# A new opening list and fewer one-column steps in a fused attention, SoLU and PReLU kernel

## Chip, cores and metric

The kernel runs on one core of one Trainium2 chip. The metric is the device time of one execution in microseconds (us). The kernel before takes 1259.91 us, the median of three runs (1259.33 to 1259.91).

## What is computed

Eight batches of eight heads, 576 positions, 64 values per head. Attention is local: each head's positions are cut in chunks of 64, and a chunk attends only to itself. Then come two dense blocks over the 4608 tokens.

```
scores = scale * q_c @ k_c^T ; attn = exp(scores - max) ; attn /= (sum(attn) + 1e-9)
x   = (attn @ v_c)  laid out as 4608 tokens x 512
h   = x @ w_in (512 x 1024) ; e = exp(h - max(h)) ; solu = h * e / (sum(e) + 1e-9)
y   = (solu - mean) / sqrt(var + 1e-6) * g_ln @ w_out (1024 x 512)
h2  = y @ w_in2 (512 x 2048) ; out = (max(h2,0) + alpha * min(h2,0)) @ w_out2 (2048 x 512)
```

## The kernel before

Each float32 product is made from rounded high parts and remainders (low parts): high x high, high x low and low x high, three matmuls. The program has two phases. Phase 1 goes over 36 token tiles of 128 and does attention, the SoLU block and the normalisation, and writes y to DRAM. Phase 2 does the second dense block, with sums of blocks in place of some of the products.

All work is issued in an order written out by hand, and each engine runs its own instructions in that order. A two-letter or one-letter name stands for one step and the number behind it for the tile or weight unit. `FIRST` is the list for the opening, up to tile 10 or so; after it `STEP` is repeated for each tile, and `LAST` drains phase 1 into phase 2. The steps that matter here, with engine and line:

- `q`, `v` load a tile (SP queue; `q` is held back until the `qk` that frees its buffer was issued, 3 buffers; `v` likewise). `f` fetches a weight unit. The weights come as 64-bit numbers; a unit is 128 x 512 of them. Units 0 to 7 are w_in, 8 to 15 are w_out, the later ones belong to phase 2.
- Conversion of unit u: `p` (ACT, L147 and L148, two activations of 128x512), `s`/`S` (subtract, L153), `l` (DVE, L159 then L162), `a`/`A` (add, L348), `h` (ACT, high part, L356, or L363 and L364), `o`/`O` (low part, L368). A small letter puts `s`, `a` and `o` on GpSimd (POOL), a capital on VectorE (DVE).
- Attention of tile i: `qk` (PE, 32 small matmuls, L381), `qm` (DVE, max L390 and subtraction L392), `qe` (ACT, exp in place, L397), `qs` (DVE: sum over 64 columns L401, plus 1e-9 L402, reciprocal L403), `qn` (e times the reciprocal, L408; on POOL for i < 12, else on DVE), `tr` (PE transposes, L415), `te` (ACT copy out of PSUM, L420), `pv` (PE, L436), `xh` (ACT, L448), `xl` (DVE, L453).
- SoLU of tile i: `hm` (PE, 24 matmuls of 512 columns, L462 and L468, into the only PSUM buffer of its kind), `hx` (DVE, max over 1024, L476), `he` (ACT, exp with the sum, L482), `so` (DVE: plus 1e-9 L487, reciprocal L488, product with the sum over the row L490, and -sum/1024 L493), `sq` (ACT, square with bias and sum, L498), `zv` (DVE, one column, L503), `pw` (POOL, power -0.5, L509), `zs` (DVE, 128x1024, L513), `zt` (PE transposes, L524), `zh` (ACT, L538), `zl` (DVE, L544).
- `ya`, `yb` (PE, L169 to L171): the second product in blocks of 12 matmuls; `ye`, `yx` copy results out (ACT, L571) and store them.

`hm` of the next tile can't start before `so` (L490) has read the PSUM buffer. The first `hm` needs all eight units of w_in: their high parts `h` and their low parts `o`, the low parts in the order in which its matmuls use them.

Of the kernel before, what the change touches and what calls it, by code (L numbers as in the profile page):

```python
# [1171 lines left out]
```

## Time and profile before

| | |
|---|---|
| median of three runs | 1259.91 us |
| profiled execution: its own time | 1258.6 us |
| profiled execution: span, first to last instruction | 1256.7 us |
| PE busy | 1223.2 us, 97% of the span |
| VectorE (DVE) busy | 926.9 us, 74% |
| ScalarE (ACT) busy | 674.9 us, 54% |
| GpSimd (POOL) busy | 324.1 us, 26% |

The profile is that of one execution, 1.3 us under the median. Busy time is the time in which an engine has an instruction in flight. Two instructions of one engine can overlap a little at their ends, so the start of one to the start of the next (a step, below) is what an instruction costs its engine. Stretches are given in us from the start of the span.

### The profile page before, as it was taken

To read this page: it belongs to the slowest core of one execution; us is meant where nothing else is said; L and a number is where in the kernel's file an instruction comes from. 1 tells how busy PE (TensorE), PEld (TensorE's weight loads), DVE (VectorE), ACT (ScalarE), POOL (GpSimd) and SP (SyncE) were. 2 spreads that over 40 slices of the span, in tenths; PEclk is the share of its full clock that TensorE was granted. 3 is DMA by queue.
4 is the path that set the end of the run, shared out by engine and by line. 5 is a ranking of instruction groups with operands and counts; after the bars stand their busy time and mean duration, and the time that the engine had idled before them with its cause. 6 is when DMAs were issued, how large, how long until landed. Compare 5 with 4: busy or idle time off the path is not lost.

```text
span 1256.7 us, 20820 instructions
## 1 busy us (share of the span) xinstructions
PE 1223.2 (97%) x7830; PEld 1058.8 (84%) x7830; DVE 926.9 (74%) x1345; ACT 674.9 (54%) x1061; POOL 324.1 (26%) x299
## 2 busy tenths in 40 slices
PE   5789999999999999999999999999999999999998
PEld 4678888888888888888888899988888888889998
DVE  7986577777877777436776777777885977859594
ACT  6685455555555555335665656666634444434442
POOL 4665145544646555233011020300000000000000
PEclk9899999999999999999999999999999999999999
DMA  8453356564745643468653445469993837547463
GB/s 329 152 158 110 102 175 184 167 197 141 243 162 186 225 168 135 146 266 329 232 201 122 153 174 164 166 233 316 327 349 119 286 112 243 179 138 246 140 213 101
DMA packets 148276, 244.63 MB, mean 195 GB/s; under 512 B 14672, under 2 KB 81360, under 8 KB 147664
## 3 DMA queue, kind: packets, MB, share of 16 engines
q1 hardware_dynamic: 145872, 241.22, 56.1%
q10 hardware_dynamic: 2304, 2.10, 0.5%
q8 instruction: 61, 1.00, 0.3%
q14 instruction: 39, 0.32, 0.1%
HBM read 154.93 MB, written 88.34 MB: 194 GB/s over the span
## 4 chain that ended last, share of the span: by engine, by line
PE 73%; issue 10%; POOL 9%; DVE 4%; ACT 3%; DMA 1%; DVEq 0%; POOLq 0%; ACTq 0%
PE ov L1010 8%; PE oz L1010 8%; PE ox L1010 8%; PE hv L767 7%; PE hx L767 7%; PE hz L767 7%; PE h L462 6%; PE oy L1010 4%; PE hy L767 3%; PE yps L169 3%; PE yps L171 3%; PE yps L170 3%; POOL lo L236 3%; PE h L468 3%; POOL a L153 2%
## 5 line engine op out<-in xcount | busy, mean ns | idle before, releaser
L806 DVE SCALAR_TENSOR_TENSOR g<-ng,nal,g 128x512 f32<-128x512 f32 (+1 forms) x160 | 117.5, 734 | 51.2 <-ACT g L679 49.5
L679 ACT ACTIVATE ng<-g 128x512 f32<-128x512 f32 (+1 forms) x120 | 70.8, 590 | 121.6 <-DVE g L673 121.1
L169 PE MATMUL yps<-zz,wo_h 128*128 128x512 f32 x288 | 115.2, 400 | 0.0
L171 PE MATMUL yps<-zz,wo_l 128*128 128x512 f32 x288 | 112.4, 390 | 0.0
L170 PE MATMUL yps<-zz,wo_h 128*128 128x512 f32 x288 | 112.2, 389 | 0.0
L767 PE MATMUL hv<-th,w 128*128 128x512 f32 (+1 forms) x320 | 104.9, 368 | 0.4 <-DVE g L673 0.3
L767 PE MATMUL hz<-th,w 128*128 128x512 f32 (+1 forms) x320 | 104.7, 368 | 0.4 <-DVE g L673 0.3
L767 PE MATMUL hx<-th,w 128*128 128x512 f32 (+1 forms) x320 | 104.7, 368 | 0.2 <-ACT g L679 0.2
L1010 PE MATMUL ov<-rhi,w 128*128 128x512 f32 (+3 forms) x308 | 93.1, 364 | 0.0
L1010 PE MATMUL oz<-rhi,w 128*128 128x512 f32 (+1 forms) x304 | 92.8, 366 | 0.0
L1010 PE MATMUL ox<-rhi,w 128*128 128x512 f32 (+1 forms) x304 | 92.8, 366 | 0.0
L679 ACT ACTIVATE rhi<-rt 128x1024 fp32r<-128x1024 f32 (+1 forms) x56 | 53.8, 969 | 62.0 <-DVE rt L676 16.8
L676 POOL TENSOR_TENSOR yt<-y,y 128x512 f32<-128x512 f32 (+1 forms) x20 | 25.8, 1310 | 216.7 <-DMA y<-yd 216.7
L676 DVE TENSOR_TENSOR rlo<-rt,rhi 128x1024 fp32r<-128x1024 f32 (+1 forms) x56 | 61.3, 1107 | 15.5 <-ACT rhi L679 15.4
L679 ACT ACTIVATE g<-g 128x512 f32<-128x512 f32 (+1 forms) x120 | 70.3, 586 | 2.6
L462 PE MATMUL h<-wi_h,xh 128*128 128x512 f32 x256 | 68.9, 391 | 0.0
L462 PE MATMUL h<-wi_l,xh 128*128 128x512 f32 x256 | 68.7, 390 | 0.0
L767 PEld LDWEIGHTS hv<-th,w 128*128 128x128 f32 x320 | 59.6, 188 | 9.1 <-issue 0.8
L767 PEld LDWEIGHTS hz<-th,w 128*128 128x128 f32 x320 | 59.6, 188 | 8.5 <-DVE g L673 1.0
L767 PEld LDWEIGHTS hx<-th,w 128*128 128x128 f32 x320 | 59.6, 188 | 8.1 <-ACT g L679 0.6
L498 ACT ACTIVATE eh<-sl,st 128x1024 f32<-128x1024 f32 x36 | 41.5, 1152 | 45.5 <-DVE st L493 45.5
L171 PEld LDWEIGHTS yps<-zz,wo_l 128*128 128x128 f32 x288 | 54.0, 188 | 11.8
(175 smaller groups left out, 3212.9 us busy)
## 6 DMA issues: line engine op xcount, KB each, us to landing
gd<-g SPq DMA_DIRECT2D x96, 256.0 KB, 3.1
qkt<-in_qk SPq DMA_DIRECT2D x36, 512.0 KB, 5.2
w<-wod SPq DMA_DIRECT2D x28, 448.0 KB, 5.0
gd<-g SPq DMA_DIRECT2D x64, 192.0 KB, 1.8
raw<-in_moe_w_out SPq DMA_DIRECT2D x24, 511.8 KB, 4.2
rc<-gd SPq DMA_DIRECT2D x22, 512.0 KB, 4.1
rd<-gd SPq DMA_DIRECT2D x22, 512.0 KB, 4.9
vt<-in_v SPq DMA_DIRECT2D x36, 256.0 KB, 4.8
```

The costliest lines, as they stand in the source:

```text
L169: nc.tensor.matmul(o, lh, rh, start=first, stop=False)
L170: nc.tensor.matmul(o, lh, rl, start=False, stop=False)
L171: nc.tensor.matmul(o, ll, rh, start=False, stop=last)
L236: nc.gpsimd.tensor_tensor(out=lo[:, :w], in0=f, in1=hi[:, :w].bitcast(F32), op=ALU.subtract)
L462: nc.tensor.matmul(ps[:, n], xh[:, kk], w[:, kk, 512 * n:512 * n + 512], start=(kk == 0 and w is wi_h), stop=False,)
L468: nc.tensor.matmul(ps[:, n], xl[:, kk], wi_h[:, kk, 512 * n:512 * n + 512], start=False, stop=(kk == K1 - 1),)
L498: nc.scalar.activation(out=e, in_=s, func=AF.Square, bias=st[:, 4:5], accum_out=st[:, 5:6])
L676: eng.tensor_tensor(out=out, in0=a, in1=b, op=ALU.subtract)
L679: nc.scalar.activation(out=out, in_=in_, func=func, **k)
L767: nc.tensor.matmul(self.ps[x], w[:, a, i, k], d[:, k], start=(p not in CHAINED and k + j == 0), stop=(k == 1 and j == 2), skip_group_check ...
L806: nc.vector.scalar_tensor_tensor(out=self.g[t], in0=self.n[t], scalar=nal_sb[:, f:f + 1], in1=self.g[t], op0=ALU.mult, op1=ALU.add)
L1010: nc.tensor.matmul(bank[key, m][:, e:f], W[2 * j + k][:, a, i, 128 * m:128 * m + 128], d[:, k, e:f], start=(p not in CHAINED and j + k + q ...
```

## The change

- `qs`: exp now writes its 64 columns per head into one of two tiles with 65 columns per head, whose last column was set to 1e-9 once. The sum goes over 65 columns, and the addition L402 is gone.
- `qn` reads that tile and writes the old one. The list says which engine: `qn` POOL, `QN` DVE. The opening list has `QN0` and `qn1` to `qn11`, `STEP` has `QN`, so only tile 0 changes engine. `qe` of a tile has to come behind `qn` of the tile two before.
- `so`: L487 now also multiplies by 1024, so that the sum of L490 is the mean, up to a power of two; L493 is gone, `sq` takes its bias straight from L490, and a new one-column POOL instruction behind `sq` makes the mean for `zs`. The factor 32 x 1024 that is then missing is put into the copy of `ye`.
- `zv` is one addition instead of a multiplication and an addition, in one instruction as before.
- Buffers: `q` has four instead of three, e of SoLU two tiles instead of one (odd tiles use the new one, on the left side of SBUF), and the two 65-column tiles are new.
- A new opening list, with the same 412 entries up to capitals. `s` on DVE: 15 instead of 8 (in the opening), `a` 8 instead of 7, `o` of units below 16: 9 instead of 4.

Lists and diff are cut behind the first `ya`:

```diff
--- before.py
+++ after.py
@@ -51,28 +51,28 @@
 FIRST_TILES = 10
 FIRST = order(
     """
-    q0 f0 p0 q1 qk0 f1 q8 qk1 qm0 f3 qe0 q9 f2 p1 qs0 s0 qn0 tr0 te0 l0 v0 a0 q2 pv0 q12 qm1 f5 p3 q7 S1
-    qe1 qk2 l1 q3 A1 f4 v1 qs1 p2 S2 h1 qm2 xh0 q4 v2 l2 h0 p5 qe2 s3 xl0 v4 qk3 qn1 o0 qs2 O1 a2 f8 p4
-    qm3 qn2 l3 tr1 v7 f7 f6 te1 h2 tr2 q5 qe3 pv1 a3 S4 v3 f10 xh1 qs3 qk4 o2 qn3 te2 p7 qm4 qe4 pv2 S5
-    l4 h16 tr3 l5 A4 xh2 q6 qs4 te3 a5 p6 s7 xl2 f9 xl1 qk5 qm5 p8 h4 v8 v5 h5 qn4 h3 s6 O4 tr4 f11 qe5
-    l6 te4 qs5 pv4 A6 xh4 l7 f12 pv3 xh3 qk6 qn5 A7 h6 h7 o6 xl3 v6 o5 qm6 o7 O3 qe6 s8 tr5 te5 xl4 qs6
-    l8 a8 hm0 p9 qn6 p10 s10 hx0 g0 qk7 qk8 he0 qm7 s9 qe7 so0 p11 l9 tr6 q10 qs7 hm1 qm8 pv5 qn7 sq0 h8
-    te6 l10 qe8 p12 zv0 qk9 a10 qs8 f13 pw0 a9 hx1 zs0 he1 s11 pv6 so1 qm9 xh5 xh6 sq1 tr7 s12 te7 xl5
-    zt0 zv1 h10 hm2 pw1 l12 f14 zh0 p13 l11 zs1 zl0 hx2 qe9 a11 pv7 a12 S13 qn8 f15 qk10 al0 zt1 o8 h11
-    o11 o10 he2 p14 tr8 so2 q11 qs9 sq2 S14 zv2 zh1 l14 pw2 f16 h9 zs2 hm3 f18 zl1 v11 a14 p15 hx3 qn9
-    l13 xl6 f21 a13 te8 h12 f17 zt2 he3 zh2 f19 p16 f20 tr9 so3 h13 zl2 sq3 qm10 hm4 s15 pv8 qk11 te9
-    l15 s16 xh7 zv3 h14 A15 p18 pw3 s18 o16 O13 o14 l16 h15 o9 hx4 o12 he4 zs3 o15 zt3 so4 sq4 zh3 l18
-    zv4 qe10 p17 zl3 A16 hm5 s17 hx5 ya1 he5 l17 yb1 so5 sq5 ye1 hm6 p19 a17 ya0 qs10 zv5 pw4 h18 xl7
...
+    q10 q0 qk0 qm0 f1 p1 f0 qe0 qs0 QN0 p0 q1 f3 S0 l0 s1 l1 qk1 a1 q2 v0 f2 qm1 v7 p3 qe1 q3 tr0 te0 p2
+    qk2 f5 h1 v4 f4 S3 A0 qs1 qm2 h16 q4 pv0 l3 S2 qn1 f6 qe2 qk3 f7 q8 l2 h0 xh0 p4 qs2 v1 a2 q12 qm3
+    tr1 te1 a3 v2 qe3 xl0 qk4 qs3 v8 v3 p5 qm4 q5 qn2 f9 h2 S4 O1 q6 S5 tr2 qe4 p6 pv1 te2 l5 o0 xh1 qn3
+    f8 l4 tr3 p7 pv2 q7 f10 A4 h4 o4 A5 S7 S6 q11 qs4 qk5 o2 qn4 xl1 te3 xh2 xl2 qm5 l7 l6 p9 tr4 qk6 h5
+    te4 qe5 A7 a6 q9 h3 qs5 h7 g0 h6 f11 p8 pv3 qm6 O6 xh3 f12 O5 qe6 f14 O7 f13 pv4 xh4 O3 v5 S8 qn5
+    xl4 l8 hm0 tr5 qs6 a8 qk7 hx0 qk8 qn6 te5 s9 qm7 he0 qe7 so0 l9 O17 a9 qs7 qm8 p10 tr6 sq0 p11 zv0
+    f16 qn7 hm1 te6 pw0 pv5 S10 S11 l10 h8 qe8 zs0 p12 hx1 v6 qk9 he1 S12 l12 so1 zt0 l11 al0 qm9 xh5
+    a10 h9 sq1 qs8 xl3 tr7 hm2 xl5 h10 zh0 o8 f17 zv1 a12 te7 zl0 a11 p14 qe9 pv6 pw1 pv7 hx2 qn8 p13
+    he2 tr8 s14 zs1 s13 so2 qk10 zt1 h12 l14 qm10 qs9 sq2 l13 a13 zv2 p16 zh1 zl1 te8 pw2 h11 hm3 hx3
+    he3 zs2 qn9 h18 f15 so3 p15 xh7 zt2 tr9 f18 sq3 S15 A14 zh2 zv3 pw3 l15 h14 zl2 h13 te9 hm4 s16 zs3
+    hx4 he4 xl7 A15 so4 qk11 l16 h15 O15 xh6 v9 pv8 zt3 h17 o13 o10 O9 f20 hm5 p18 sq4 o11 S18 zh3 xl6
+    v10 zl3 zv4 hx5 he5 so5 O14 p17 O12 ya1 qe10 ya2 sq5 f19 hm6 v11 S17 xh8 pw4 l17 a16 l18 f21 zs4 zv5
...
     """
 )
 STEP = order(
     """
     q+3 v+3 ye-6 zh-2 zl-2 conv+0 hm+0 tr+1 te+1 qk+2 hx+0 he+0 qm+2 qe+2 pv+1 zt-1 so+0 sq+0
-    ya-5 xh+1 xl+1 zv+0 pw+0 conv+1 qs+2 zs+0 qn+2 yb-5 yx-5
+    ya-5 xh+1 xl+1 zv+0 pw+0 conv+1 qs+2 zs+0 QN+2 yb-5 yx-5
     """
 )
 TWICE = {20, 26, 31}
@@ -174,13 +174,13 @@
         with ExitStack() as c1, ExitStack() as c0:
             L = lambda name, bufs, **k: c0.enter_context(tc.tile_pool(name=name, bufs=bufs, side="left", **k))
             R = lambda name, bufs, **k: c1.enter_context(tc.tile_pool(name=name, bufs=bufs, side="right", **k))
-            qkp = L("qk", 3)
+            qkp = L("qk", 4)
...
-            ep = R("e", 1)
+            ep = R("e", 1), L("f", 1)
@@ -194,7 +194,7 @@
 -            frees = {"q": ("qk", 3), "v": ("pv", 3)}
+            frees = {"q": ("qk", 4), "v": ("pv", 3)}
 
             def load_q(i):
                 t = qs[i] = qkp.tile([128, 2, 2, 2, 2, CH], F32, name="qkt", tag="qk")
@@ -368,6 +368,9 @@
                 eng.tensor_tensor(out=units[u][2] if u < UI else wo["l"][:, u - UI], in0=f, in1=hi.bitcast(F32), op=ALU.subtract)
 
             sc, ee, att, xs, hs = {}, {}, {}, {}, {}
+            exs = [at.tile([128, H, CH + 1], F32, name=f"ex{k}", tag=f"ex{k}", bufs=1) for k in range(2)]
+            for ex in exs:
+                nc.gpsimd.memset(ex[:, :, CH:CH + 1], 1e-9)
             ss, zz_, pvs, rs = {}, {}, {}, {}
 
             def qk(i):
@@ -393,19 +396,22 @@
                 ee[i, 0] = e
 
             def qexp(i):
+                assert i < 2 or ("qn", i - 2) in done
                 e = ee[i, 1] = ee.pop((i, 0))
-                nc.scalar.activation(out=e, in_=e, func=AF.Exp, scale=scale)
+                nc.scalar.activation(out=exs[i % 2][:, :, 0:CH], in_=e, func=AF.Exp, scale=scale)
 
             def qsum(i):
+                assert ("qe", i) in done
                 r = sm.tile([128, H], F32, name="r", tag="r", bufs=3)
-                nc.vector.tensor_reduce(out=r, in_=ee[i, 1], op=ALU.add, axis=AX.X)
-                nc.vector.tensor_scalar(out=r, in0=r, scalar1=1e-9, scalar2=None, op0=ALU.add)
+                nc.vector.tensor_reduce(out=r, in_=exs[i % 2], op=ALU.add, axis=AX.X)
                 nc.vector.reciprocal(out=r, in_=r)
                 rs[i] = r
 
-            def qnorm(i):
+            def qnorm(i, eng):
                 e, r = ee[i, 1], rs.pop(i)
-                (nc.gpsimd if i < 12 else nc.vector).tensor_tensor(out=e, in0=e, in1=r.unsqueeze(2).to_broadcast([128, H, CH]), op=ALU.mult)
+                eng.tensor_tensor(
+                    out=e, in0=exs[i % 2][:, :, 0:CH], in1=r.unsqueeze(2).to_broadcast([128, H, CH]), op=ALU.mult
+                )
 
             def tr(i):
                 assert i not in rs
@@ -478,30 +484,34 @@
 
             def hexp(i):
                 st = ss.pop((i, 0))
-                e = ep.tile([128, FF1], F32, name="eh", tag="eh")
+                e = ep[i % 2].tile([128, FF1], F32, name="eh", tag="eh")
                 nc.scalar.activation(out=e, in_=hs[i], func=AF.Exp, bias=st[:, 0:1], accum_out=st[:, 1:2])
                 ss[i, 1] = st, e
 
             def solu(i):
                 st, e = ss.pop((i, 1))
-                nc.vector.tensor_scalar(out=st[:, 2:3], in0=st[:, 1:2], scalar1=1e-9, scalar2=None, op0=ALU.add)
+                nc.vector.tensor_scalar(
+                    out=st[:, 2:3], in0=st[:, 1:2], scalar1=1e-9, scalar2=float(FF1), op0=ALU.add, op1=ALU.mult
+                )
                 nc.vector.reciprocal(out=st[:, 2:3], in_=st[:, 2:3])
                 s = sp.tile([128, FF1], F32, name="sl", tag="sl")
                 nc.vector.scalar_tensor_tensor(
                     out=s, in0=hs.pop(i), scalar=st[:, 2:3], in1=e, op0=ALU.mult, op1=ALU.mult, accum_out=st[:, 3:4]
                 )
-                nc.vector.tensor_scalar(out=st[:, 4:5], in0=st[:, 3:4], scalar1=-1.0 / FF1, scalar2=None, op0=ALU.mult)
                 ss[i, 2] = st, e, s
 
             def square(i):
                 st, e, s = ss.pop((i, 2))
-                nc.scalar.activation(out=e, in_=s, func=AF.Square, bias=st[:, 4:5], accum_out=st[:, 5:6])
+                nc.scalar.activation(
+                    out=e, in_=s, func=AF.Square, scale=-float(FF1), bias=st[:, 3:4], accum_out=st[:, 5:6]
+                )
+                nc.gpsimd.tensor_scalar(out=st[:, 4:5], in0=st[:, 3:4], scalar1=1.0 / FF1, scalar2=None, op0=ALU.mult)
                 ss[i, 3] = st, s
 
             def zvar(i):
                 st, s = ss[i, 4] = ss.pop((i, 3))
                 nc.vector.tensor_scalar(
-                    out=st[:, 6:7], in0=st[:, 5:6], scalar1=1.0 / FF1, scalar2=1e-6, op0=ALU.mult, op1=ALU.add
+                    out=st[:, 6:7], in0=st[:, 5:6], scalar1=1e-6 * FF1, scalar2=None, op0=ALU.add
                 )
 
             def zpow(i):
@@ -511,7 +521,7 @@
             def zscale(i):
                 st, s = ss.pop((i, 5))
                 nc.vector.tensor_scalar(
-                    out=s, in0=s, scalar1=st[:, 4:5], scalar2=st[:, 7:8], op0=ALU.add, op1=ALU.mult
+                    out=s, in0=s, scalar1=st[:, 4:5], scalar2=st[:, 7:8], op0=ALU.subtract, op1=ALU.mult
                 )
                 zz_[i] = s
 
@@ -568,7 +578,7 @@
 
             def ystore(j, m):
                 y = yp.tile([128, YG], F32, name="ysb", tag="ysb")
-                nc.scalar.activation(out=y, in_=ypend.pop((j, m)), func=AF.Copy)
+                nc.scalar.activation(out=y, in_=ypend.pop((j, m)), func=AF.Copy, scale=32.0 * FF1)
                 pairs = (0, 1) if Z_SLOTS[j][0][0] < Z_SLOTS[j][1][0] else (1, 0)
                 for c, p in enumerate(pairs):
                     t0 = j * YG + p * YP
@@ -594,21 +604,21 @@
             nc.gpsimd.memset(b64[:, 0:1], -8.0 * 896 * 16)
             nc.gpsimd.memset(b64[:, 1:2], -8.0 * (896 + 2048) * 16)
             nc.gpsimd.memset(mhalf, -0.5)
-            nc.scalar.activation(out=mhalf, in_=mhalf, func=AF.Copy)
+            nc.scalar.activation(out=b64, in_=b64, func=AF.Copy)
             make_identity(nc, ident)
...
-                qk=qk, qm=qmax, qe=qexp, qs=qsum, qn=qnorm, tr=tr, te=tevac, pv=pv, xh=xhigh, xl=xlow,
+                qk=qk, qm=qmax, qe=qexp, qs=qsum, qn=lambda i: qnorm(i, nc.gpsimd), QN=lambda i: qnorm(i, nc.vector), tr=tr, te=tevac, pv=pv, xh=xhigh, xl=xlow,
...
```

## Rows read from the trace of the kernel before

**Rows 1.** Windows: engines' busy time in stretches, granted TensorE clock, DMA

```profile
0.00:43.50 43.50, 24.04 (x408) 21.41 (x409) 32.89 (x61) 26.59 (x44) 20.24 (x26) 0.88 0.77 285
...
80.00:90.00 10.00, 6.79 (x30) 5.49 (x29) 9.76 (x19) 9.54 (x17) 4.62 (x5) 0.83 0.40 122
...
101.36:560.00 458.64, 456.47 (x3580) 384.88 (x3579) 320.74 (x531) 243.70 (x395) 222.41 (x208) 1.00 0.52 174
```

Columns: stretch and its length; busy time and (x instructions) of PE, PE weight loads, DVE, ACT and POOL; granted TensorE clock as a share of full speed; share of the DMA engines' time; GB/s.

**Rows 2.** Timeline of PE: where the `hm` groups and the first `ya` begin

```profile
43.50 1.17 PE L462 MATMUL h<-wi_h,xh 128*128 128x512 f32 x4
...
53.70 1.21 PE L462 MATMUL h<-wi_h,xh 128*128 128x512 f32 x4
...
74.17 1.16 PE L462 MATMUL h<-wi_h,zz 128*128 128x512 f32 x4 [1.04 <-DVE sl L490]
...
84.40 2.04 PE L462 MATMUL h<-wi_h,zz 128*128 128x512 f32 x4 [3.21 <-DVE sl L490]
...
95.83 1.15 PE L462 MATMUL h<-wi_h,zz 128*128 128x512 f32 x4 [1.09 <-DVE sl L490]
...
101.36 0.39 PE L169 MATMUL yps<-zz,wo_h 128*128 128x512 f32 x1
```

Columns: start, duration, engine, line, operation, output and inputs, shape, number merged; in brackets the idle time before it and what ended it.

**Rows 3.** Timeline: the links between the first and second `hm`

```profile
49.46 1.23 DVE L476 TENSOR_REDUCE st<-h 128x1 f32<-128x1024 f32 x1 [0.17 <-PE h L468]
...
50.72 1.11 ACT L482 ACTIVATE eh<-h,st 128x1024 f32<-128x1024 f32 x1 [1.14 <-DVE st L476]
...
52.35 1.28 DVE L490 SCALAR_TENSOR_TENSOR sl<-h,st,eh 128x1024 f32<-128x1024 f32 x1
```

**Rows 4.** Windows: the stretch from the first `qm` to the first `hx`

```profile
7.30:49.46 42.16, 28.02 (x402) 24.05 (x404) 38.55 (x69) 28.20 (x48) 24.14 (x21) 0.88 0.72 274
```

**Rows 5.** Timeline of DVE in the opening

```profile
16.35 0.70 DVE L402 TENSOR_SCALAR r<-r 128x8 f32<-128x8 f32 x1
...
17.20 0.39 DVE L153 TENSOR_TENSOR a<-pos,neg 128x512 bf16<-128x512 bf16 x1
17.51 0.68 DVE L390 TENSOR_REDUCE nm<-sc 128x8 f32<-128x512 f32 x1
18.22 0.69 DVE L392 TENSOR_TENSOR e<-sc,nm 128x512 f32<-128x512 f32 x1
18.83 1.04 DVE L159 TENSOR_SCALAR g<-a 128x512 uint16<-128x512 uint16 x1
19.91 0.69 DVE L162 SCALAR_TENSOR_TENSOR f<-wrawh,g 128x512 f32<-128x512 uint32 x1
20.52 0.68 DVE L453 TENSOR_TENSOR xl<-xd,xh 128x512 fp32r<-128x512 f32 x1
21.12 0.68 DVE L401 TENSOR_REDUCE r<-e 128x8 f32<-128x512 f32 x1
21.83 0.17 DVE L402 TENSOR_SCALAR r<-r 128x8 f32<-128x8 f32 x1
22.03 0.20 DVE L403 RECIPROCAL r<-r 128x8 f32<-128x8 f32 x1
22.15 0.64 DVE L368 TENSOR_TENSOR wi_l<-f,wi_h 128x512 fp32r<-128x512 f32 x1
...
24.14 0.28 DVE L159 TENSOR_SCALAR g<-a 128x512 uint16<-128x512 uint16 x1
```

**Rows 6.** Timeline of POOL beside the first row of Rows 5

```profile
15.87 1.16 POOL L153 TENSOR_TENSOR a<-pos,neg 128x512 bf16<-128x512 bf16 x1 [2.29 <-DVE f L348]
```

**Rows 7.** Waits of PE up to 101 us: who waited for whom, total, times, longest

```profile
PE et L415 <- POOL e L408: 8.0, 4, 4.4
```

**Rows 8.** Timelines of SP, ACT and PE around the start of phase 2

```profile
525.79 2.03 SPq L724 DMA_DIRECT2D y<-yd  x4
...
529.66 1.15 ACT L498 ACTIVATE eh<-sl,st 128x1024 f32<-128x1024 f32 x1 [2.00 <-DVE st L493]
...
559.69 0.39 PE L767 MATMUL hx<-y,w 128*128 128x512 f32 x1
```

More of the change, by code (lines that the diff above doesn't have):

```diff
@@ L64 @@
-    l15 s16 xh7 zv3 h14 A15 p18 pw3 s18 o16 O13 o14 l16 h15 o9 hx4 o12 he4 zs3 o15 zt3 so4 sq4 zh3 l18
-    zv4 qe10 p17 zl3 A16 hm5 s17 hx5 ya1 he5 l17 yb1 so5 sq5 ye1 hm6 p19 a17 ya0 qs10 zv5 pw4 h18 xl7
-    zs4 xh8 pw5 f22 hx6 zt4 zh4 he6 yb0 zs5 a18 zt5 zl4 h19 ya2 xl8 hm7 p20 so6 S19 zh5 s20 ye0 v9 sq6
-    zl5 zv6 pw6 pv9 zs6 hx7 he7 so7 p21 sq7 zt6 yb2 zh6 hm8 v12 v10 xh9 h17 zv7 xl9 l19 o18 hx8 pw7 zl6
-    qn10 tr10 a19 zs7 qm11 o17 te10 he8 ya3 yb3 zt7 so8 pv10 sq8 zh7 zl7 hm9 l20 f23 ya4 zv8 hx9 S21 ye3
@@ L69 @@
-    he9 pw8 ye2 yx3 xh10 A20 zs8 so9 sq9 qe11 zv9 qs11 pw9 xl10 qn11 zs9 yb4 zt8
+    q10 q0 qk0 qm0 f1 p1 f0 qe0 qs0 QN0 p0 q1 f3 S0 l0 s1 l1 qk1 a1 q2 v0 f2 qm1 v7 p3 qe1 q3 tr0 te0 p2
+    qk2 f5 h1 v4 f4 S3 A0 qs1 qm2 h16 q4 pv0 l3 S2 qn1 f6 qe2 qk3 f7 q8 l2 h0 xh0 p4 qs2 v1 a2 q12 qm3
+    tr1 te1 a3 v2 qe3 xl0 qk4 qs3 v8 v3 p5 qm4 q5 qn2 f9 h2 S4 O1 q6 S5 tr2 qe4 p6 pv1 te2 l5 o0 xh1 qn3
+    f8 l4 tr3 p7 pv2 q7 f10 A4 h4 o4 A5 S7 S6 q11 qs4 qk5 o2 qn4 xl1 te3 xh2 xl2 qm5 l7 l6 p9 tr4 qk6 h5
@@ new lines @@
+    he3 zs2 qn9 h18 f15 so3 p15 xh7 zt2 tr9 f18 sq3 S15 A14 zh2 zv3 pw3 l15 h14 zl2 h13 te9 hm4 s16 zs3
+    hx4 he4 xl7 A15 so4 qk11 l16 h15 O15 xh6 v9 pv8 zt3 h17 o13 o10 O9 f20 hm5 p18 sq4 o11 S18 zh3 xl6
+    v10 zl3 zv4 hx5 he5 so5 O14 p17 O12 ya1 qe10 ya2 sq5 f19 hm6 v11 S17 xh8 pw4 l17 a16 l18 f21 zs4 zv5
+    hx6 he6 yb1 pw5 zs5 xl8 zt4 ya0 ye1 zh4 A17 so6 a18 hm7 yb0 zl4 qs10 o18 zt5 qm11 p19 sq6 ye0 pv9
+    hx7 zv6 pw6 zh5 he7 p20 zs6 zl5 yb2 qn10 so7 zt6 hm8 ya3 ye2 sq7 yb3 zh6 zv7 S19 pw7 l19 s20 xh9 zl6
@@ L70 @@
+    hx8 xl9 he8 zs7 tr10 p21 qe11 zt7 zh7 l20 so8 qs11 hm9 sq8 te10 f22 pv10 h19 zv8 pw8 zl7 hx9 yx3 he9
+    v12 ya4 zs8 so9 a19 xh10 zt8 ye3 xl10 o16 qn11 sq9 zv9 pw9 s21 A20 zs9 yb4 f23
     """
@@ L119, in tile_chunk_attention_solu_prelu @@
     al_sb = const.tile([128, KF2], F32, name="al_sb")
-    mhalf = const.tile([128, 1], F32, name="mhalf")
-    b64 = const.tile([128, 2], F32, name="b64")
+    b64 = const.tile([128, 3], F32, name="b64")
+    mhalf = b64[:, 2:3]
     y_dram = [dram.tile([128, K1, 2 * n], F32, name=f"yd{j}") for j, (_, n) in enumerate(GROUP)]
@@ L196, in phase1 @@
             done = set()
-            frees = {"q": ("qk", 3), "v": ("pv", 3)}
+            frees = {"q": ("qk", 4), "v": ("pv", 3)}
             def load_q(i):
@@ L610, in phase1 @@
             top = dict(
-                {k: TILES for k in "q v qk qm qe qs qn tr te pv xh xl hm hx he so sq zv pw zs zt zh zl ya yb ye yx".split()},
+                {k: TILES for k in "q v qk qm qe qs qn QN tr te pv xh xl hm hx he so sq zv pw zs zt zh zl ya yb ye yx".split()},
                 **{k: len(units) for k in "fpsla"}, **{k: UO for k in "hoO"}, S=len(units), A=len(units), g=1, al=1,
```

## Prediction, made before the changed kernel was run

> **What bounds the kernel now.** The windows come first [rows 1]: up to 43.5 us PE is busy 24.04 us only, so it idles 19.5; from 80 to 90 it idles 3.2; from 101.36 to 560, 458.64 us, it idles 2.2. So behind the first `ya` PE's own work sets the pace, and that work is the same in both kernels. What the change can win or lose is the time of the fifth `hm` interval's end, 95.83, or of the first `ya`, 101.36 [rows 2]; from there every microsecond is carried to the end, and nothing else on DVE, ACT or POOL shows.
>
> Next, the timeline of PE [rows 2]: the `hm` groups of tiles 0 to 5 begin at 43.50, 53.70, (the third not shown,) 74.17, 84.40 and 95.83: 10.2, twice 10.2, 10.2 and 11.4 us. The links [rows 3] say what an interval is: `hm` itself 5.7 to 6.0 (43.50 to 49.46), from `hx` to `he` 1.26, to the product of `so` 1.63, to the next `hm` 1.35. That is a loop through one PSUM buffer, PE to DVE to ACT to DVE to PE. A change that takes none of these four instructions away can't make it much shorter than 10.2. So the opening has two parts: A, how soon the first `hm` ends and `hx` starts (49.46), and B, five intervals (46.4 us).
>
> Part A is set by DVE. From its first instruction at 7.30 to `hx` at 49.46 DVE is busy 38.55 of 42.16 us [rows 4], and `hx` starts 0.17 us behind the end of `hm`: both were late together. PE's waits in that stretch are for POOL's `qn` (8.0 us [rows 7]), which is filled from DVE in turn.
>
> **Step prices on DVE.** From start to start, undisturbed [rows 5]: `S` 0.31 (17.20 to 17.51), `qm` 0.71 + 0.61, `l` 0.31 + 0.61 (L159 takes 0.28 and 0.03 to the next), `xl` 0.60, `qs` 0.71 + 0.20 + 0.12, of which L402 is the 0.20. I take `A` and `QN` at 0.61 like L162 and `O` at 0.60 like `xl`, all operations on 512 float32 columns.
>
> Some are disturbed. L402 at 16.35 takes 0.70, not 0.17, and ends at 17.05, when POOL's subtraction (15.87 plus 1.16 [rows 6]) ends; L159 at 18.83 takes 1.04 instead of 0.28 [rows 5]. So some DVE instructions wait for the POOL instruction in flight. The Trainium skill (SBUF — State Buffer, Who interferes with whom) says the same and more: a DVE instruction with two inputs in SBUF, too, shares a port with GpSimd, and whichever starts first keeps it for its whole length. By that rule every `S`, `A`, `O` and `QN` that is moved to DVE is one more candidate to wait; the sum with that stands among the rivals, worked out from L402's row.
>
> **Part A, list against list.** Ahead of `hx0` the old list has on DVE 7 `qm`, 7 `qs`, 9 `l`, 4 `S`, 4 `A`, 3 `O`, 5 `xl`: 9.24 + 7.21 + 8.28 + 1.24 + 2.44 + 1.80 + 3.00 = 33.2 us. The new one has 7 `qm`, 7 `qs` (now 0.83), 9 `l`, 8 `S`, 4 `A`, 5 `O`, 4 `xl` and `QN0`: 9.24 + 5.81 + 8.28 + 2.48 + 2.44 + 3.00 + 2.40 + 0.61 = 34.3. DVE gets 1.05 us more to do, since 4 `S`, 2 `O` and `QN0` outweigh L402 seven times. (65 columns instead of 64 are a sixty-fourth of 0.71, 0.01 each.)
>
> So the gain has to come from the waits. Before they were 42.16 - 33.2 = 9.0 us: 3.6 idle (42.16 - 38.55), the other 5.4 inside of instructions, behind POOL. POOL has 21 instructions in this stretch [rows 4]; the new list leaves it 14: `s0`, `s3`, `s6`, `s7`, `s8`, `a0`, `a5`, `qn0`, `o5`, `o6`, `o7` go to DVE or behind `hx0`, and `s1`, `a1`, `o4`, `a6` come. Two estimates, from above and below:
> - Waits behind POOL fall with the count, 14/21, and the idle time stays: 34.3 + 3.6 + 3.6 = 41.5, `hx0` at 48.8.
> - Walking down the new list entry by entry with these prices, 1.16 for a POOL instruction [rows 6] and somewhat over half of 1.15 for an ACT instruction of 512 columns (1.15 is one of 1024 [rows 8]), DVE waits in four places only: for the first exp 0.7 (as before), for `qk2` 0.35, for `qe3` 0.15, `S4` behind POOL's `qn3` 0.55. Together 1.75: DVE is at `hx0` at 7.30 + 34.3 + 1.75 = 43.4. `O3` ends at 40.7, and `hm0` needs it for 11 of its 24 matmuls (0.23 us each: 95.83 to 101.36 is 24 of them), so `hm0` ends at about 43.7. `hx0` at 43.7. The q and f loads don't hold this up: `f6` and `f7` stand before `v1` now, and q's fourth buffer lets `q3` go without `qk0`.
>
> A walk sees no delays that add up, a proportion doesn't see that the list was laid out anew. I take the middle, 46.25: 3.2 us earlier than 49.46. The ends stay for the range (0.7 and 5.8).
>
> **Part B.** L493 lies behind the product that releases `hm` and `he`, `hx` and the product stay: the loop stays 10.2. In the walk three intervals get longer: `qm7` waits for `qk7` behind `tr5`, which was moved behind `hm0` (0.35); `S10`, `S11` and `zs0` stand ahead of `hx1` (0.15); ACT has 11 instructions of 512 columns (`h9`, `h10`, `p13`, `p14`, `te7`, `qe9`, `xh5`), `sq1` and `zh0` between `he1` and `he2`, with `he` some 10.6 us of work for 10.2 (0.4). Against it stands the fifth interval: PE idled 3.2 us before 84.40, and then the granted clock fell to 0.83 for that stretch [rows 1], between the levels of 1.2 and 2.4 GHz; the first four matmuls took 2.04 instead of 1.16 [rows 2], and the interval 1.2 us more. In the new list `zs2` stands behind `hx3`, so `zt2` falls into the middle of that gap and cuts it in two; I take the 1.2 as won. Part B: 0.9 lost, 1.2 won, 0.3 gained, less 0.1 for what a walk misses: 0.2.
>
> **What costs nothing, and what covers it.** POOL's new one-column instruction: at most the 1.16 of 512 columns [rows 6], ahead of `pw`, which waits for `zv` anyway. If POOL were late it would delay `zs`, then `zt`, which PE's `ya` work covers behind 101.36. `S`, `A` and `O` behind `hx5`: DVE's work grows by some 3 us up to tile 9, against PE groups of 5.5 us and `ya` blocks between them. `O12` and `O14` stand behind `so5`, but only `yb1`, behind `hm6`, uses these units. `zv`, `ye`: same instruction, other constants. `STEP`: 0.28 us less on DVE per tile, where PE doesn't wait. `qe` behind `qn` of two tiles before: in the walk `qn` is done over 3 us ahead. The memory layout grows by 12 KB on the left, so phase 2's second and third y transfer (issued at 525.79) may land where the odd e tile lies and then wait for the last square, which ends at 530.8 [rows 8]. SP and the weights behind it are up to 5 us later; PE wants the first y at 559.69, 34 us after the issue. Zero, and up to 5 us if that cover were gone.
>
> **Sum.** 3.2 + 0.2 = 3.4 us. The profiled execution took 1258.6 (span 1256.7, 1.9 around it), so 1255.2 by its account; it stands 1.3 under the median, so against the median of 1259.91: **1256.5 us**. 0.2% (2.5 us) is about what a measurement of this kernel can tell from no change.
>
> **Rivals.**
> 1. *The walk holds in full*: `hx0` at 43.7, 5.8 + 0.2 = 6.0, 1253.9 us. For it: fewer POOL instructions, and DVE ones that don't meet them. Against it: the same prices leave 9.0 us unexplained before.
> 2. *No change.* L402's wait is not L402's: it is handed to the next instruction that needs POOL to be done, and the idle time moves. Waits stay 9.0, DVE gets 1.05 more, B gives its 1.2 back at the clock: 1259.8 us. For it: DVE is at 38.55 of 42.16 and its own work doesn't shrink. The change then does what it says, but saves only a carrier of waits.
> 3. *Slower*: each DVE instruction moved from POOL waits for the POOL instruction in flight, 0.53 each as L402 did (0.70 against 0.17). Ahead of `hx0` these are 4 `S`, 2 `O` and `QN0`: 7 x 0.53 = 3.7, plus 1.05 of work: 4.8 us, 1264.7 us. That is the port rule of the Trainium skill (the page above) with every instruction losing. It decides from where DVE's waits ahead of `hx0` are over 9.0 - 1.05 = 8.0 us. Against it: POOL is left 14 instructions of 21, so there are fewer to run into.
>
> **Chances.** Forecast (1255.0 to 1258.6) 0.43, rival 1 0.15, rival 2 0.27, rival 3 0.15. Faster by over 0.2% (below 1257.4) are rival 1 and nine tenths of the forecast: 0.54. Within 0.2%: rival 2 and the rest of the forecast, 0.31. Slower: 0.15. The range takes in the forecast, rival 2 and most of rival 1, leaves out the greater part of rival 3: 1253.4 to 1261.0. The forecast's own range is 1255.0 to 1258.6.
>
> **What would show it.** Right: `hx0` at 45 to 48, DVE's waits from 7.30 to there about 4.7 us; `hm` intervals 10.2 to 10.6, all with first matmuls of 1.2, not 2.0; fewer L159 and L153 on DVE that end with a POOL instruction; no PE idle behind the first `ya` beyond the 2.2 us. Wrong: `hx0` at 48.5 or later; a slow group of `hm` again; DVE rows stretched by POOL (rival 3); PE waiting between `hm5` and the end of tile 9, or at the start of phase 2.

## The result and the profile after the change

| | before | after |
|---|---|---|
| median, lowest to highest (6 runs each) | 1259.88 us, 1259.04 to 1260.04 | 1269.35 us, 1268.39 to 1271.94 |
| ratio, 95% interval | | 1.0078, 1.0065 to 1.0091 |
| profiled execution, its span | 1258.6, 1256.7 us | 1268.5, 1266.3 us |

The change costs 9.5 us; a gain of 3.4 was forecast. Windows of the changed kernel, to set beside the last two of [rows 1] (stretch, length, busy time and count of PE, weight loads, DVE, ACT, POOL, granted clock, DMA share, GB/s):

```profile
80.00:90.00 10.00, 7.92 (x58) 6.37 (x60) 7.21 (x14) 8.14 (x13) 3.99 (x6) 1.00 0.25 80
99.51:559.06 459.55, 457.82 (x3578) 384.68 (x3576) 314.43 (x477) 245.58 (x398) 232.16 (x240) 1.00 0.52 174
```

And its timeline of PE, to set beside [rows 2]:

```profile
41.68 1.35 PE L468 MATMUL h<-wi_h,xh 128*128 128x512 f32 x4
...
52.30 1.20 PE L468 MATMUL h<-wi_h,xh 128*128 128x512 f32 x4
...
73.40 1.16 PE L468 MATMUL h<-wi_h,zz 128*128 128x512 f32 x4
...
83.58 1.17 PE L468 MATMUL h<-wi_h,zz 128*128 128x512 f32 x4 [0.73 <-DVE sl L498]
...
93.83 1.17 PE L468 MATMUL h<-wi_h,zz 128*128 128x512 f32 x4 [1.39 <-DVE sl L498]
...
99.51 0.39 PE L169 MATMUL yps<-zz,wo_h 128*128 128x512 f32 x1
```

In this execution the opening did what it was meant to: the first `hm` begins at 41.68 instead of 43.50, the slow group at 84.40 is gone (1.17 us at a granted clock of 1.00, not 2.04 at 0.83), the first `ya` begins at 99.51 instead of 101.36. That is 1.85 us gained. But from there to phase 2 it took 459.55 us, before 458.1 (101.36 to 559.46), and from phase 2 to the end 707.24 (1266.3 less 559.06), before 697.24. Losses of 1.45 and 10.0, less the gain: 9.6 us, the difference of the spans. PE has no idle time to show for them. Phase 2 goes over eight weight units, b0 to b7, with 42 matmuls each. Its first group of 512 columns, first in the kernel before, then in the changed one; the first line is b0 and b1, the second the six units b2 to b7, 252 matmuls from the first start to the next group's first:

```profile
559.46:578.50 19.04, 19.04 (x85) 15.77 (x84) 12.34 (x17) 9.98 (x18) 0.00 (x0) 1.00 0.70 239
578.51:635.63 57.12, 57.12 (x254) 47.30 (x253) 42.93 (x59) 35.55 (x60) 12.14 (x8) 1.00 0.78 289
```

```profile
559.06:578.13 19.07, 19.07 (x85) 15.77 (x84) 12.35 (x17) 9.98 (x18) 0.00 (x0) 1.00 0.67 229
578.13:636.92 58.79, 58.79 (x253) 47.34 (x252) 43.13 (x59) 35.98 (x60) 12.19 (x8) 1.00 0.79 284
```

PE is busy to the last hundredth in all four. (Its count takes in the matmuls that overlap the ends.) Units b0 and b1 take the same time; b2 to b7 take 58.79 us where they took 57.12. From start to start a matmul of 512 columns takes 226.7 ns in every unit before; after, 226.7 to 227.3 in b0 and b1 and 233.3 in b2 to b7. The granted clock is 1.00 in all, the weight loads take the same (47.30 and 47.34 us in b2 to b7), the DMA share is alike. Matmuls of 384 columns step as before, at 173 ns.

**Where they lie.** An edit that the diff ahead shows only in part: the one-column constant `mhalf` became the third column of `b64`.

```
-    mhalf = const.tile([128, 1], F32, name="mhalf")
-    b64 = const.tile([128, 2], F32, name="b64")
+    b64 = const.tile([128, 3], F32, name="b64")
+    mhalf = b64[:, 2:3]
```

In these programs a 4-byte tile takes 32 bytes a partition (`mhalf` at 1248, `b64` at 1280), so every tile behind it on the left of SBUF now starts 32 bytes lower; those on the right stay. The new `ex` tiles, 2080 bytes each, move `wi_h` and `wi_l` by another 64. Start addresses modulo 512 in the two programs:

```
                       before  after
xh, xl, th, tl, w20-1  288     256     (left)
wi_h, wi_l             288     320     (left)
zz, wo_h, wo_l, w22-7  288     288     (right)
```

Before, both operands of every matmul of 384 or 512 columns start at the same residue, that is, at the same remainder. (The stationary operand of a matmul is the 128x128 of its weight load, the moving one has the 384 or 512 columns. A difference below is moving less stationary start.) After, those of b2 to b7 (moving `th`, `tl`, stationary `w22` to `w27`) differ by -32, `hm` of tiles 2 to 5 (`zz`, `wi`) by +32 and steps at 234 ns, the other `hm` (`xh`, `wi`) by +64 and step at 229. Estimate: 42 matmuls a unit, 6 units, 3 groups of 512 columns make 756, the last stage's three 512-column chunks with 252 each as many again: 1512 times 6.6 ns is 10.0 us, and 10.0 were lost in phase 2. The theory: **a matmul's step depends on the difference of its operands' start addresses.** The rival: the list and the instructions put other work beside PE.

### The profile page after: what moved, and what is told of

It reads as the page before. It is cut to its first block, busy times and chain, and to the rows that moved or that the text cites. A ratio compares the mean times of both kernels' runs of the same rounds, so it can differ in the third digit from the quotient of the medians.

```text
span 1266.3 us, 20763 instructions
## 1 busy us (share of the span) xinstructions
PE 1234.3 (97%) x7830; PEld 1058.8 (84%) x7830; DVE 919.7 (73%) x1287; ACT 675.8 (53%) x1061; POOL 316.6 (25%) x323
## 4 chain that ended last, share of the span: by engine, by line
PE 88%; DVE 2%; issue 1%; ACT 1%; POOL 1%; DVEq 0%; POOLq 0%
PE h L468 8%; PE ov L1020 8%; PE oz L1020 8%; PE ox L1020 8%; PE hv L777 7%; PE hz L777 7%; PE hx L777 7%; PE yps L169 5%; PE yps L171 5%; PE yps L170 5%; PE h L474 4%; PE oy L1020 4%; PE hy L777 4%; PE zt L534 2%; PE xd L442 2%; PE sc L384 2%
## 5 line engine op out<-in xcount | busy, mean ns | idle before, releaser
L554 DVE TENSOR_TENSOR zz<-zt,zz 128x1024 fp32r<-128x1024 f32 x36 | 44.0, 1221 | 31.8 <-ACT zz L548 31.8
```

What stands on the lines that cost most here:

```text
L554: nc.vector.tensor_tensor(out=zl, in0=ps, in1=zh.bitcast(F32), op=ALU.subtract)
```

## The experiments

**Four layouts.** Each adds an unused tile or makes the merge alone; "right -32" is built from the changed kernel and from the one before.

```
after, left +32:   +    const.tile([128, 1], F32, name="gap")
right -32 (both):  +    ctx.enter_context(tc.tile_pool(name="edge", bufs=1, side="right")).tile([128, 8], F32, name="edge")
before, merged:    -    mhalf = const.tile([128, 1], F32, name="mhalf")
                   -    b64 = const.tile([128, 2], F32, name="b64")
                   +    b64 = const.tile([128, 3], F32, name="b64")
                   +    mhalf = b64[:, 2:3]
```

> The changed kernel with one unused tile of 4 bytes a partition (32 allocated) behind b64, nothing else: every buffer on the left of SBUF starts 32 bytes higher, so that it lies at 32 modulo 64 again, as in the kernel before and as the buffers on the right do. Theory (addresses: a matmul is slower where its stationary and its moving operand start at different residues modulo 64): the 512-column matmuls of phase 2 go back from 233.3 to 227.0 ns a step in all eight units, hm2 to hm5 from 234 to 227, and the time falls to about 1258 us, 1.9 us under the kernel before, since the first ya at 99.5 instead of 101.4 us stays. Rival (the loss comes from the list and the instructions: other transfers or evictions beside PE's matmuls): 32 bytes change nothing, 1269 us and 233 ns stay.

> The changed kernel with one unused tile of 32 bytes a partition at the far end of the right side: left stays at 0 modulo 64, the right side moves from 32 to 0 modulo 64 too. Theory (it is the difference of the two operands' residues that counts): all eight weight units and hm2 to hm5 step at 226 to 227 ns, some 2 us may stay because wi_h then differs from xh and zz by 64 modulo 128; 1257 to 1260 us. Rival (a start at 0 modulo 64 is slow in itself, whichever operand): b2 to b7 stay at 233 ns and b0, b1 join them, 1269 us or more. Rival (list and instructions): 1269 us.

> The kernel before with the one part of the change that makes mhalf the third column of b64, all else old: the buffers on the left move down by 32 bytes, to 0 modulo 64. Theory (addresses): phase 2 loses 9.8 us (233 instead of 227 ns for units b2 to b7), hm some 2 us: 1270 to 1272 us. Rival (list and instructions): the merge only saves a tile, 1260 us and 227 ns throughout.

> The kernel before with one unused tile of 32 bytes a partition at the far end of the right side: left stays at 32 modulo 64, right moves to 0 modulo 64. Theory (the difference counts): the same units as in the merged one, b2 to b7 and hm2 to hm5, step at 233 ns, 1269 to 1272 us. Rival (a start at 0 modulo 64 is slow in itself, for the moving operand alone): no change, 1260 us, since the moving operands of phase 2 lie on the left. Rival (32 modulo 64 is slow in itself): faster than 1260.

| | median | ratio to before, 95% |
|---|---|---|
| after, left +32 | 1258.81 | 0.9997, 0.9988 to 1.0006 |
| after, right -32 | 1258.29 | 0.9994, 0.9985 to 1.0003 |
| before, merged | 1269.94 | 1.0084, 1.0070 to 1.0098 |
| before, right -32 | 1273.41 | 1.0113, 1.0099 to 1.0126 |

An unused tile of 32 bytes takes the whole loss away, on either side, and the merge alone, with old list and old instructions, brings all of it. One window of phase 2 tells them apart, PE's count for 100 us (443 in the kernel before, 432 in the changed one). The two changed kernels, left +32 and right -32:

```profile
600.00:700.00 100.00, 100.00 (x443) 82.84 (x442) 74.69 (x105) 62.07 (x103) 9.21 (x8) 1.00 0.49 175
```

```profile
600.00:700.00 100.00, 100.00 (x443) 82.79 (x442) 75.16 (x106) 62.34 (x104) 9.21 (x8) 1.00 0.49 173
```

The two kernels of before, merged and right -32:

```profile
600.00:700.00 100.00, 100.00 (x433) 80.93 (x432) 73.28 (x103) 62.23 (x104) 9.24 (x8) 1.00 0.50 175
```

```profile
600.00:700.00 100.00, 100.00 (x433) 80.79 (x432) 74.20 (x104) 61.97 (x103) 9.31 (x8) 1.00 0.50 175
```

In the two changed kernels phase 2 has all its operands at 32 modulo 64 (left +32) or all at 0 (right -32), and both are fast: it isn't the address but the difference.

The last kernel came out 1.4 us above its expectation, which counted matmuls of 512 columns alone. Its trace shows where: with moving less stationary at +32 those of 384 columns slow down too. Units b2 to b7 of the first group of 384 columns, 252 matmuls, in the merged kernel (-32), then in this one (+32):

```profile
731.61:775.32 43.71, 43.71 (x254) 43.65 (x253) 33.33 (x58) 27.75 (x58) 9.40 (x8) 1.00 0.47 162
```

```profile
732.29:776.81 44.52, 44.52 (x253) 44.52 (x253) 33.89 (x58) 28.10 (x58) 9.44 (x8) 1.00 0.47 162
```

That is 173.5 and 176.7 ns a step, and phase 2 takes 710.0 us there against 707.5.

**The size of the difference.** 64 bytes more on the left of the kernel before (first line), and in the changed kernel with left +32, 64 bytes ahead of `wi_h` (second), which I then thought would bring `wi` and `xh` to the same class.

```
+    const.tile([128, 16], F32, name="gap")
+            L("gap2", 1).tile([128, 16], F32, name="gap2")
```

> The kernel before with 64 unused bytes a partition more on the left: every buffer on the left moves, but stays at 32 modulo 64; against the right side it now differs by 64 modulo 128. Theory (32 modulo 64 of difference costs 6.5 ns, 64 modulo 128 a third of it): units b2 to b7 step at 229 to 230 ns, phase 2 loses some 3.5 us, 1262 to 1264 us. Rival (only the residue modulo 64 counts): 227 ns, 1259.6 us. Rival (any move of the buffers upsets phase 2): 1269 us.

> The changed kernel with the left side back at 32 modulo 64 and another 64 unused bytes ahead of wi_h and wi_l, so that they start at the same residue modulo 128 as xh, xl and zz (32; before this pad they were at 96). Theory (a difference of 64 modulo 128 costs a matmul some 2 to 3 ns): hm's steps behind the first ya fall from 230 to 227 ns, from there to phase 2 some 458 instead of 459.8 us, and the time is 1256 to 1257.5 us, the fastest of all kernels here. Rival (only the residue modulo 64 counts, and the 1.5 us that phase 1 lost come from something in the list): steps and stretch stay, 1258.5 us like the kernel with the left side at 32 alone.

The first took 1263.98 us (1.0038, 1.0024 to 1.0052). Its b2 to b7 in the first group of 512 columns:

```profile
580.71:638.39 57.68, 57.68 (x253) 47.33 (x252) 43.08 (x59) 35.66 (x60) 12.11 (x8) 1.00 0.78 287
```

That is a step of 229 ns: 64 bytes cost a third of what 32 do, as expected. The second took 1263.68 (1.0032, 1.0020 to 1.0043) where 1256 to 1257.5 was expected: a miss. Its `wi` differ from `xh` and `zz` by 128, and that was not "the same class". The second half of an `hm`, 8 matmuls, with differences of 64 (left +32) and of 128:

```profile
66.47 2.00 PE L475 MATMUL h<-wi_h,zz 128*128 128x512 f32 x8
```

```profile
66.28 2.02 PE L476 MATMUL h<-wi_h,zz 128*128 128x512 f32 x8
```

Less 0.39 us for the last matmul, and divided by 7, that is 230 and 233 ns a step. Modulo 128 was wrong.

**The cost by itself.** TensorE alone, in one execution: one group of 32 matmuls for each offset, that is, moving less stationary start in bytes.

> Measures the disputed cost by itself, computes nothing of the reference: TensorE alone, no DMA and no other engine beside it, groups of 32 matmuls (128x128 stationary, 128x512 moving, fp32r, each with its weight load, eight stationary and four moving slices in turn), one group for each offset between the moving and the stationary start address modulo 512 bytes: 0, 32, 64 ... 480, then 0, 4 and 16, then both shifted together by 32, 64, 128, then the stationary alone by 32, 64, 128, then the moving alone by 512. Theory (the difference of the two start addresses counts, inside TensorE's own reads): 227 ns a step at 0, 512 and where both are shifted, 233 at 32 and 480, 229 to 230 at 64, 233 to 235 at 128, the same for the stationary shifted. Rival (the cost arises only beside the traffic of DMA and the other engines): one step at all offsets. Rival (absolute addresses): the groups shifted together differ from the first.

Windows of this kernel, each from the first start of a group to that of the next. In order of the lines: offsets 0, 32, 64, 96, 128; 192, 224, 256, 320; 0 again, 4, 16, both shifted by 32, by 64; the stationary alone by 32, by 64:

```profile
32.58:39.84 7.26, 7.26 (x33) 6.01 (x32) 0.00 (x0) 0.60 (x1) 0.00 (x0) 1.00 0.10 36
39.84:47.31 7.47, 7.47 (x33) 6.00 (x32) 0.00 (x0) 0.00 (x0) 0.00 (x0) 1.00 0.00 0
47.31:54.64 7.33, 7.33 (x33) 6.01 (x32) 0.00 (x0) 0.00 (x0) 0.00 (x0) 1.00 0.00 0
54.64:62.12 7.48, 7.48 (x33) 6.01 (x32) 0.00 (x0) 0.00 (x0) 0.00 (x0) 1.00 0.01 2
62.12:69.58 7.46, 7.46 (x33) 6.01 (x32) 0.00 (x0) 0.00 (x0) 0.00 (x0) 1.00 0.00 0
...
77.07:84.54 7.47, 7.47 (x33) 6.01 (x32) 0.00 (x0) 0.00 (x0) 0.00 (x0) 1.00 0.00 0
84.54:92.01 7.47, 7.47 (x33) 6.01 (x32) 0.00 (x0) 0.00 (x0) 0.00 (x0) 1.00 0.01 2
92.01:99.28 7.27, 7.27 (x33) 6.01 (x32) 0.00 (x0) 0.00 (x0) 0.00 (x0) 1.00 0.00 0
...
106.75:114.09 7.34, 7.34 (x33) 6.01 (x32) 0.00 (x0) 0.00 (x0) 0.00 (x0) 1.00 0.00 0
...
151.45:158.73 7.28, 7.28 (x33) 6.01 (x32) 0.00 (x0) 0.00 (x0) 0.00 (x0) 1.00 0.00 0
158.73:166.32 7.59, 7.59 (x33) 6.08 (x32) 0.00 (x0) 0.00 (x0) 0.00 (x0) 1.00 0.00 0
166.32:173.73 7.41, 7.41 (x33) 6.01 (x32) 0.00 (x0) 0.00 (x0) 0.00 (x0) 1.00 0.00 0
173.73:181.02 7.29, 7.29 (x33) 6.01 (x32) 0.00 (x0) 0.00 (x0) 0.00 (x0) 1.00 0.01 2
181.02:188.30 7.28, 7.28 (x33) 6.01 (x32) 0.00 (x0) 0.00 (x0) 0.00 (x0) 1.00 0.00 0
...
195.60:203.06 7.46, 7.46 (x33) 6.01 (x32) 0.00 (x0) 0.00 (x0) 0.00 (x0) 1.00 0.00 0
203.06:210.52 7.46, 7.46 (x33) 6.02 (x32) 0.00 (x0) 0.00 (x0) 0.00 (x0) 1.00 0.01 2
```

The length by 32 is the step: 226.9 ns at 0, 227.2 at 256; 229.1 at 64, 229.4 at 320; 233 to 234 at every other multiple of 32, those not shown and that of -64 (the last line) among them; 237 at 4 bytes, 232 at 16. Shifted together, 227.5 to 227.8. DMA and the other engines all but stand still in it, so the cost needs no other traffic: it is TensorE's own. Which part of TensorE loses the time isn't shown. The offset counts modulo 256.

**The repair.** The same pad made 448 bytes, so that `wi` differs from `xh` and `zz` by 512.

```
-            L("gap2", 1).tile([128, 16], F32, name="gap2")
+            L("gap2", 1).tile([128, 112], F32, name="gap2")
```

> The changed kernel with the left side back at 32 modulo 64 and 448 unused bytes ahead of wi_h and wi_l (in place of 64), so that they stand to xh, xl and zz at a multiple of 512 bytes, as all operand pairs of the kernel before do. Theory (a difference of 64 modulo 512 costs 3 ns, 128 costs 6, 0 nothing): hm's steps 227 ns, 458 us from the first ya to phase 2, 1256.5 to 1257.5 us, the fastest kernel here. Rival (the place of wi_h matters in another way, so that any pad ahead of it costs): 1262 us or more.

1255.73 us (1255.36 to 1258.62, 7 runs), ratio 0.9974, 0.9963 to 0.9985: with its operands lined up the change gains 4.0 us on the kernel before, measured beside it (1259.68), and is faster than both. That is 0.8 below what was expected. Its windows from the first `ya` to phase 2, then the same stretch with a difference of 128 (the pad of 64 bytes):

```profile
97.39:555.36 457.97, 456.18 (x3578) 384.51 (x3576) 314.12 (x477) 245.57 (x398) 231.89 (x240) 1.00 0.53 174
```

```profile
99.06:561.52 462.46, 460.99 (x3577) 384.64 (x3576) 314.46 (x477) 245.84 (x398) 232.28 (x240) 1.00 0.52 173
```

457.97 us, as 458.1 before the change; so the 1.45 us that phase 1 lost were `hm`'s too.

**List or instructions?** Four kernels, two with the pad of 64 bytes (against 1263.68) and two with that of 448 (against 1255.73). Their edits are hunks of the change, undone: the old opening list; the old bodies of the softmax and SoLU steps, or of the softmax alone, in the new layout.

```
-                nc.vector.tensor_reduce(out=r, in_=exs[i % 2], op=ALU.add, axis=AX.X)
+                nc.vector.tensor_reduce(out=r, in_=ee[i, 1], op=ALU.add, axis=AX.X)
+                nc.vector.tensor_scalar(out=r, in0=r, scalar1=1e-9, scalar2=None, op0=ALU.add)
...
```

> The same kernel (all buffers at 32 modulo 128) with the old opening list and the new instructions. Theory (as in the prediction, DVE's waits behind POOL are what the list saves, the new instructions save 0.2 us a qs): first hx at 48 to 49.5, first ya at 100 to 101, with the slow hm group at 84 us back, 1258.5 to 1259.5 us. Rival (the instructions give the gain): first ya at 99.5 as with the new list, 1257 us.

> The same kernel with the new opening list and the old instructions: the sum's 1e-9 as an instruction of its own, e normalised in place, SoLU's minus-mean on DVE, no scale at the y eviction (the buffers and their addresses as in the new one). Theory (the list gives the gain): first ya at 99.5 to 100.2, 1257 to 1258 us. Rival (the instructions give it): first ya at 101 or later, 1259 us; rival 2 of the prediction (each L402 that goes only hands its wait on) expects no difference to the new instructions.

> The kernel just named with the old softmax alone (the sum's 1e-9 as a DVE instruction of its own, e in place), SoLU as in the change. Theory (what the opening gains is mostly this instruction, 0.4 us on average and up to 0.7 where it stands behind a POOL instruction): first ya some 1.5 to 2 us later, 1258.5 to 1259.5 us. Rival (SoLU's step between the product and the next instructions gives the gain): no difference, 1257 us.

> The kernel with 448 unused bytes ahead of wi_h (all operand pairs at a multiple of 512 bytes) and the new instructions, but with the old opening list. Theory (the instructions give the opening's gain, the list some 0.4 us of it): first ya at 97.5 to 98.5 us, 1255.7 to 1257 us. Rival (as the prediction's part A had it, the list gives it): first ya at 100 us or later, 1258.5 us or more.

| | median | against the same pad | first `ya` |
|---|---|---|---|
| old list, pad 64 | 1263.56 | -0.1 | 99.45 (99.06) |
| old instructions, pad 64 | 1264.73 | +1.1 | 101.52 (99.06) |
| old softmax, pad 448 | 1258.60 | +2.9 | 98.96 (97.39) |
| old list, pad 448 | 1258.53 | +2.8 | 101.41 (97.39) |

The last column is of one execution each; those of the old list with pad 64 and of its partner were 2.3 us under their medians, that of the old softmax 2.65. Only the old softmax came out as its theory had it; the first `ya` of the other three is their rivals'. With the old instructions (pad 64) the added one on DVE waits as it did before [rows 5], up to 0.70 us where 0.17 is the undisturbed time:

```profile
54.40 0.70 DVE L407 TENSOR_SCALAR r<-r 128x8 f32<-128x8 f32 x1
```

The two old lists contradict each other. With the pad of 448 the slow `hm` group is back, behind 3.22 us of idle PE, and its interval takes 12.2 us instead of 10.1. With that of 64 (the second fence) the same idle time is there, but all six groups of that execution begin with 1.16 to 1.19:

```profile
83.69 2.05 PE L470 MATMUL h<-wi_h,zz 128*128 128x512 f32 x4 [3.22 <-DVE sl L500]
...
95.86 1.16 PE L470 MATMUL h<-wi_h,zz 128*128 128x512 f32 x4 [0.59 <-DVE sl L500]
```

```profile
83.45 1.17 PE L470 MATMUL h<-wi_h,zz 128*128 128x512 f32 x4 [3.21 <-DVE sl L500]
```

The gap is the list's; what the clock makes of it differs between executions. All six profiled executions with the old list have 3.2 us of idle PE ahead of the fifth `hm`, and in five of them the granted clock from 80 to 90 us is 0.83, in this one 1.00. In the seven with the new list the gap is 0.5 to 0.7 us, and the clock is 0.83 in one.

With the pad of 448 either part costs 2.8 to 2.9 us when it is missing, so there both are needed for the 4.0. Whether the two add up isn't shown: the intervals of these ratios are about 0.1% (1.2 us) either way. The -0.1 and +1.1 of the pad of 64 don't settle it. What the list alone is worth, between 0 and 2.8, stays open.

## Why the prediction was wrong

**The step that failed** is "that work is the same in both kernels": the matmuls are the same, their step is not. Under "What costs nothing" the new layout was priced by its size (12 KB, the y transfer, up to 5 us), not by where operands start. That transfer made nobody wait: PE goes into phase 2 at 559.06, before at 559.46. Missing from the sum were 10.0 us in phase 2 and 1.45 in phase 1. Nearly all that was listed as signs of "right" came true: `hx0` at 47.65, intervals of 10.2 to 10.6, no slow group, no more PE idle behind the first `ya` than before. Of the signs of "wrong" only rows on DVE stretched by POOL showed, at a small price (below). All of them are waits, and a slower step is none. The rival on the slower side had the sign but not the mechanism.

**Part A** was 1.8, not 3.2, and for another reason than the layout. The first `hx` of the changed kernel and what is ahead of it on DVE:

```profile
45.95 0.20 DVE L407 RECIPROCAL r<-r 128x8 f32<-128x8 f32 x1
47.65 1.22 DVE L482 TENSOR_REDUCE st<-h 128x1 f32<-128x1024 f32 x1 [1.50 <-PE h L474]
```

DVE was ready at 46.15, against the forecast's 46.25. That it came so close is luck, since 46.25 was the middle of two estimates 5 us apart. DVE's waits from its first instruction (6.96) to there, 4.9 us by the prediction's prices, are near the 4.7 forecast. But PE came 1.50 later, so the bound had moved from DVE to PE; "Part A is set by DVE" no longer held. PE's waits up to 110 us, first of the kernel before (`qn`'s are in [rows 7]), then of the changed one:

```profile
PE sc L381 <- DMA qkt<-in_qk: 5.3, 1, 5.3
...
PE sc L381 <- issue: 3.4, 2, 1.8
```

```profile
PE sc L384 <- DMA qkt<-in_qk: 7.5, 2, 4.9
PE sc L384 <- issue: 5.0, 3, 2.3
...
PE et L421 <- POOL e L412: 2.0, 1, 2.0
```

The wait for `qn` fell from 8.0 to 2.0, and 3.8 of it came back as waits for q and for issue. "The q and f loads don't hold this up" doesn't fit these rows. How much of the 1.50 is theirs isn't shown: the last long wait ahead of the first `hm` is still the 2.0 for `qn`.

**DVE's waits behind POOL** fell. By the prediction's prices those inside instructions were 5.4 us and are now 1.9 (DVE is busy 36.2 us up to `hx0`, less 34.3 of work), between the proportion's 3.6 and the walk's 0.55. Groups of DVE up to the first `hx`, before and after:

```profile
L159 DVE TENSOR_SCALAR g<-a 128x512 uint16<-128x512 uint16 x9 | 4.1, 455 | 0.1
...
L402 DVE TENSOR_SCALAR r<-r 128x8 f32<-128x8 f32 x7 | 3.1, 444 | 0.2
```

```profile
L153 DVE TENSOR_TENSOR a<-pos,neg 128x512 bf16<-128x512 bf16 x8 | 4.6, 589 | 0.0
...
L159 DVE TENSOR_SCALAR g<-a 128x512 uint16<-128x512 uint16 x9 | 2.6, 290 | 0.3
```

L159 is back near its undisturbed 280 ns. L402, priced at 0.20 seven times (1.4 us), had taken 3.1 in all: the mean of its group says more than its best row. Of the eight `S` ahead of `hx0` (four of them moved from POOL) six take 0.41 to 0.42 us. The other two started while a POOL instruction was in flight, and took 0.71 and 1.50. The first of these and the POOL instruction beside it:

```profile
25.64 0.71 DVE L153 TENSOR_TENSOR a<-pos,neg 128x512 bf16<-128x512 bf16 x1
```

```profile
25.03 1.04 POOL L412 TENSOR_TENSOR e<-ex,r 128x512 f32<-128x512 f32 x1
```

So the third rival's mechanism is there, with 1.4 us over eight instructions, 0.2 each instead of 0.53. It agrees with the rule cited there (the Trainium skill, SBUF — State Buffer, Who interferes with whom), at a price that gave little away here.

**Part B** held as a number: from the first to the sixth `hm` 52.15 us (41.68 to 93.83) against 52.33 before, 0.18 gained for a forecast of 0.2, and no slow group. In part that is luck: the slow group comes back in the kernel with left +32, which has the same list (2.05 us at 83.05), and three of the five intervals have an `hm` that the layout made some 0.16 us longer (24 times 6.6 ns). In the repaired kernel the first and the sixth `hm` begin at

```profile
40.89 1.20 PE L470 MATMUL h<-wi_h,xh 128*128 128x512 f32 x4
...
91.86 1.16 PE L470 MATMUL h<-wi_h,zz 128*128 128x512 f32 x4 [1.39 <-DVE sl L500]
```

That is 2.6 us gained ahead of the first and 1.4 between the two. The whole gain there, 4.0, is near the forecast's 3.4, but its parts are not those of the forecast (3.2 and 0.2). Both are of one execution.

## What to carry to other kernels

Where a change adds, drops or resizes a tile, work out where the tiles behind it land, also when it is one column: here the merge of one 4-byte tile cost 10 us, and the edits were worth 4.0. Where matmuls of 512 columns set the pace, keep stationary and moving operands at a multiple of 256 bytes from one another, as here, and read the step between matmuls that run without idle time, not only waits: a slower step shows in no list of waits and leaves PE just as busy. A small instruction behind a contended engine is priced by the mean of its group.
